# Loading v by heads over all 128 partitions, with key groups of eight units

## The chip, the cores and the metric

The kernel runs on one core of a Trainium2 chip. The metric is the device time of one execution in microseconds. Besides the times of plain executions there is one execution that the hardware profiler recorded; all views below come from it.

## The reference

Four batches, four heads, 1,088 positions, head size 32. Queries and keys go through a small feature map (two projections to 8 numbers and all 64 products of them), the attention is linear, and its result feeds one feed-forward layer with a swish whose slope `beta` is learned for each of 2,048 hidden units.

```python
def phi(x):                                   # 64 features of each position
    a = np.einsum('rd,bhsd->bhsr', S1, x)     # r = 8
    b = np.einsum('rd,bhsd->bhsr', S2, x)
    return np.einsum('bhsi,bhsj->bhsij', a, b).reshape(*x.shape[:-1], r * r)
q_p, k_p = phi(q), phi(k)
kv = np.einsum('bhsf,bhsd->bhfd', k_p, v)
z = np.sum(k_p, axis=2)
num = np.einsum('bhsf,bhfd->bhsd', q_p, kv)
den = np.einsum('bhsf,bhf->bhs', q_p, z)[..., None] + 1e-06
x = (num / den).transpose(0, 2, 1, 3).reshape(4 * 1088, 128)
h = x @ w_in                                  # 128 -> 2048
out = (h / (1 + np.exp(-beta * h))) @ w_out   # 2048 -> 128
```

## The kernel before

**Positions and units.** The 1,088 positions of a head are numbered as 32 rows (t) of 34 consecutive positions each; "unit" u of 0 to 33 is the u-th position of every row, so a unit is 32 positions of each head. q and k are loaded with heads and rows on the 128 partitions (L168 to L173), and VectorE (DVE) transposes them in blocks of 32 by 32 (L343, L348), after which unit u of all heads is a block of 32 columns in `kT` and `qT`. Column block 34 of `kT` is a pad of zeros.

**Key groups.** The sum over positions for kv wants positions on the partitions. The key projection (`k_project`, L353) therefore writes four groups of units to the four 32-partition quarters of a PSUM tile: `KU` gives the first unit of group j and `KN` how many it has (9, 9, 8, 8). It is one fp32 matmul per group and per half e of the heads, 8 in a batch, each of 9 x 32 = 288 columns; the ninth block of the two last groups is never used. `k_turn` (L365) transposes that into `tk`, the products of the two projections (`kp`, L370 to L383) are made on GpSimd (POOL) or DVE, and `kv_sum` (L515) adds v against them: for every column group c of 0 to 8 and every head h one fp32 matmul, over 128 partitions for c < 8 and over the first 64 for c = 8. v must lie as the key groups lie: partition 32 j + t, head h, column c holds row t of unit `KU[j] + c`. `load_v` (L175) does this with one load for each quarter j:

```python
KU = (0, 9, 18, 26)
KN = (9, 9, 8, 8)
```

Each is 32 partitions by 4 heads of one run of 1,152 or 1,024 bytes. Two buffers hold v: one for batch 0, one for batches 1 to 3.

**The rest of a batch.** `z_sum` (L385), the weights for the denominator (`w_project`, `w_mask`), the query projection, the denominator (`den_product` and what follows, L471 to L498), the query products (`qp`) and their turn (`qpt`), the kv tile turned to feed the numerator (`kvw`, `kvt`, `kvc` in batch 0; `kvo` and three small copies on SP's queue in the other batches), `num` (L560) and three copies into `xall` in fp16.

**The feed-forward stage** takes `xall` in chunks of up to 512 columns: steps `f<s>a/b` multiply by `winb` (w_in times beta, made on POOL by steps `wb0` to `wb3`, L310) into a PSUM wave, ScalarE (ACT) applies the swish, and steps `s<s>a/b` multiply by `woutp` (w_out over beta, steps `wo0` to `wo3`, L313). DVE transposes finished chunks and SP's queue stores them (`o0` to `o9`).

**Order.** Every step has a name, and one hand-written list, `ORDER`, sets in which order the steps are issued; each engine and each queue takes its own part of it in that order. `lv<b><j>` is the load of quarter j of v for batch b; `lk`, `lq`, `li`, `lo`, `lba` are the loads of k, q, w_in, w_out and the broadcast beta. All of these go out on SP's queue, S1, S2 and a small copy of beta on ACT's. Steps `i<n>` are n matmuls on zeros that keep TensorE (PE) running. For batch 0 the list has, on PE, `kpj0` (key projection), `zs0`, `qpjx0`, `cpjx0`, `kv00`, `i5`, `kv30 kv10 kv20`, `kvt0`, `i7`, `numx0`; on SP's queue `lk0a lk0b lq0a lv02 li0 lv00 lv01 lv03 lk11 lba1 li2 lk10 lba0 lo0 lq0b li1 lo1`.

Of the kernel before, what the change touches and what calls it, by code (L numbers as in the profile page):

```python
# [13 lines left out]
T = 32  # L14
# [3 lines left out]
def kernel(  # L18
# [12 lines left out]
    nc = tc.nc  # L31

    B, H, S, D = q.shape
# [5 lines left out]
    U = S // T  # L39
# [2 lines left out]


    NC = 9
    KU = (0, 9, 18, 26)
    KN = (9, 9, 8, 8)
    G = NC * H
    N = NC * T

# [1 line left out]

    ORDER = """
    lk0a ls2 lk0b lq0a ident pads warm i3 lv02 li0 lv00 ls1 lb i4 zms tbl lv01 sp kta0 masks ktb0 i2 sbd lv03
    qt0x0 kpj0 ktn0 sel kp10 sp2 kp30 bt i2 s2s lk11 lba1 li2 kp20 bc i3 kp00 zs0 lk10 zc0 qpjx0 wp0 wm0 i1 i2
    lba0 qtnx0 cpjx0 kv00 rb i5 ctnx0 kv30 kv10 kv20 kvw0 kvt0 dpx0 lo0 dsx0 drx0 anx0 qp00 lq0b li1 i7 kvc0 lo1
    qp10 qpt10 qpt00 lba3 lba2 ktb1 numx0 qt00 lq11 cpj0 lq10 xcx0 kta1 li3 qpj0 wb0 wo0 wb1 xax0 xbx0 wo1 i1
    f0a f0b ctn0 f1a qtn0 lo2 wb2 f1b lk21 dp0 lk20 ds0 kpj1 dr0 an0 f2a qp30 f2b s0a qp20 f3a f3b lv11 s0b s1a
    lo3 qt01 s1b s2a s2b lv13 qpt30 ktn1 qt11 wb3 f4a f4b f5a s3a qpt20 wo2 s3b f5b zs1 qpj1 qtn1 lv10 f6a zc1
    s4a wp1 wm1 f6b kp01 s4b wo3 num0 xb0 xc0 kta2 cpj1 xa0 lq20 f7a lq21 lv12 f7b kp21 s5a f8a kp31 s5b f8b
    ktb2 s6a ctn1 s6b s7a f9a kp11 f9b s7b lk30 f10a f10b kpj2 kv31 kv21 kv11 kv01 dp1 lk31 ds1 dr1 f11a f11b  # L60
    an1 qp21 o0 f12a s8a qt02 kvo1 f12b kr21 s8b kr31 ktn2 qp01 s9a s9b qpt21 qpt01 s10a f13a f13b s10b s11a
    qp11 qpt11 kr11 qt12 s11b f14a kp02 s12a f14b s12b f15a s13a lv23 s13b ktb3 f15b zs2 num1 zc2 lv21 s14a xc1
    s14b lq31 xa1 xb1 kp32 s15a lv20 lv22 s15b f16a f16b f17a kta3 wp2 f17b qpj2 wm2 cpj2 f18a f18b kp22 kp12
    qtn2 ctn2 f19a dp2 f19b lq30 kpj3 kv12 kv22 f20a o1 ds2 f20b dr2 s16a an2 f21a f21b kv02 qp02 kv32 f22a f22b
    s16b s17a f23a kvo2 f23b s17b s18a qpt02 s18b f24a f24b s19a kr22 s19b f25a qp12 f25b s20a s20b s21a lv30
    f26a f26b kr32 ktn3 qpt12 qp22 s21b s22a f27a f27b s22b s23a qpt22 s23b f28a f28b lv32 kr12 zs3 num2 zc3 xb2
    o2 wp3 xa2 f29a f29b xc2 lv31 s24a s24b kp33 f30a lv33 f30b s25a kp03 s25b qt13 s26a wm3 s26b f31a qt03 f31b
    s27a f32a f32b cpj3 qpj3 f33a f33b f34a s27b s28a f34b s28b s29a s29b f35a kp23 f35b s30a ctn3 s30b f36a
    qtn3 kp13 f36b dp3 ds3 s31a kv23 dr3 kv13 f37a f37b s31b o3 f38a an3 f38b kv03 qp13 kv33 f39a f39b kvo3 s32a
    s32b qp23 f40a kr23 f40b s33a s33b s34a f41a f41b kr13 qp03 s34b s35a f42a f42b s35b s36a s36b f43a kr33  # L70
    f43b s37a s37b qpt03 f44a f44b s38a qpt13 qpt23 s38b s39a f45a f45b s39b num3 xb3 o4 f46a f46b s40a xa3 xc3
    f47a f47b s40b s41a s41b f48a f48b s42a s42b f49a f49b s43a s43b f50a f50b s44a s44b s45a f51a f51b s45b
    s46a f52a f52b s46b s47a s47b f53a f53b f54a o5 xr f54b s48a s48b s49a f55a f55b s49b s50a f56a f56b s50b
    s51a f57a f57b s51b s52a s52b f58a f58b s53a s53b f59a f59b s54a s54b s55a s55b f60a f60b f61a o6 f61b s56a
    s56b s57a s57b f62a f62b s58a s58b f63a f63b s59a s59b o7 s60a f64a f64b s60b s61a f65a f65b s61b s62a s62b
    f66a f66b s63a s63b o8 f67a f67b s64a s64b s65a s65b s66a s66b s67a s67b o9
    """

    ENGINES = {
# [20 lines left out]
    def ct(shape, dtype, name):  # L100
        return const.tile(shape, dtype, tag=name, name=name)
# [6 lines left out]
    v_in = [v_two[0]] + [v_two[1]] * (B - 1)  # L108
# [17 lines left out]
    kT = ct([P, U + 1, T], F32, "kT")  # L126
    qT = ct([P, U + 2, T], F32, "qT")
    prods = [ct([P, G, R + 1], F32, f"prod{i}") for i in range(2)]
    sbd = ct([P, 2, 2 * R], F32, "sbd")
# [11 lines left out]
    st = [dict() for _ in range(B)]  # L141
# [3 lines left out]
    def step(name, f, *args):  # L145
        ops[name] = lambda: f(*args)
# [25 lines left out]

        nc.sync.dma_start(out=t[i:P:2, :], in_=rows[i:P:2, :])  # L173

    def load_v(b, j):  # L175
        nc.sync.dma_start(
            out=v_in[b][T * j : T * j + T, :, 0 : KN[j], :].rearrange("p h c d -> p h (c d)"),
            in_=bass.AP(
                tensor=v.tensor,
                offset=v.offset + b * H * S * D + KU[j] * D,  # L180
                ap=[[U * D, T], [S * D, H], [1, KN[j] * D]],
            ),
        )

    def load_w_in(i):
        nc.sync.dma_start(out=w_in_sb[:, i * 512 : i * 512 + 512], in_=moe_w_in[:, i * 512 : i * 512 + 512])
# [16 lines left out]
            step(f"lk{b}{i}", load_half, k_in[b], k_rows[b], i)  # L203
            step(f"lq{b}{i}", load_half, q_in[b], q_rows[b], i)
    for b in range(B):
        for j in range(4):
            step(f"lv{b}{j}", load_v, b, j)
    for i in range(4):
        step(f"li{i}", load_w_in, i)
        step(f"lo{i}", load_w_out, i)  # L210
# [142 lines left out]
    def k_project(b, js):  # L353
        st[b]["kpp"] = att2_t("kpp")
        for j in js:
            for e in range(2):
                nc.tensor.matmul(  # L357
                    out=st[b]["kpp"][T * j : T * j + T, e, 0:N],
                    lhsT=sbd[64 * e : 64 * e + 64, :, :].rearrange("p e r -> p (e r)"),
                    rhs=kT[64 * e : 64 * e + 64, KU[j] : KU[j] + NC, :].rearrange("p u t -> p (u t)"),  # L360
                    start=True,
                    stop=True,
                )

    def k_turn(b):  # L365
        tk = sb.tile([P, G, 2 * R], F32, tag="tk", name="tk")
# [229 lines left out]
    for b in range(B):  # L596
        step(f"kta{b}", k_transpose, b, 0, 18)
        step(f"ktb{b}", k_transpose, b, 18, U)
        step(f"kpj{b}", k_project, b, range(4))
        step(f"ktn{b}", k_turn, b)  # L600
        step(f"zs{b}", z_sum, b)
# [41 lines left out]
    u = 0  # L643
# [164 lines left out]
```

## Time and profile before

| | |
|---|---|
| median of 3 executions | 104.43 us (102.4 to 105.1) |
| the profiled execution | 103.5 us, span 101.8 us, granted TensorE clock 0.995 |
| PE busy | 95.1 us, 93% of the span |
| ACT, DVE, POOL busy | 72.3, 60.3, 40.6 us |
| DMA | 12.56 MB in 24,253 packets |
| v loads | 8 of 144 KB and 8 of 128 KB, 3.8 us from issue to landing at the median |
| first kv product | 10.44 us after the span's start |
| first feed-forward wave | 18.05 us |

The span is the part of the execution that the profile records; times in it count from its start. PE, ACT, DVE, POOL and SP are engines; "PEld" is the loading of weights into PE, beside its matmuls; an fp32 matmul shows as two records, one for each of two passes. The chain of waits follows the last work of the kernel back from step to step. A row of the stretches gives, after the two times, for PE, PEld, DVE, ACT and POOL the busy time and the number of instructions, then the granted clock, the busy share of the 16 DMA engines and GB/s.

### The profile page before, as it was taken

The numbers are of one execution on the slowest core, as the hardware profiler recorded it, in microseconds if no ns is written. First come the engines' busy times: TensorE is split into PE (matmuls) and PEld (weight loads), VectorE is DVE, ScalarE is ACT, GpSimd is POOL, SyncE is SP. The second block draws the span as 40 slices with busy tenths as digits, with TensorE's granted clock in tenths as the row PEclk, the third lists the DMA queues.
The fourth block names the chain that finished last, engine by engine and source line by source line (L and its number), as shares of the span: only waits on it lengthen the run. The fifth ranks groups of instructions, "written<-read, shape, count | busy, mean of one in ns | idle before, by whom it ended". The sixth has DMA issues, their size and how long they took to land.

```text
span 101.8 us, 3167 instructions
## 1 busy us (share of the span) xinstructions
PE 95.1 (93%) x1342; PEld 48.3 (47%) x1342; DVE 60.3 (59%) x110; ACT 72.3 (71%) x92; POOL 40.6 (40%) x49
## 2 busy tenths in 40 slices
PE   5999889999999999999999999999999999999940
PEld 1244454343545446345445534454444446689930
DVE  1574997999799894798983769189351040021110
ACT  1430022687587685788996788899969999989930
POOL 6419599769997996006272000068000000000000
PEclk9999999999999999999999999999999999999998
DMA  2999999981780627712440054034003205003421
GB/s 43 343 233 257 395 378 410 377 261 45 188 279 29 103 53 191 195 54 50 76 125 10 13 93 116 0 56 81 5 13 52 45 9 94 0 17 66 74 55 52
DMA packets 24253, 12.56 MB, mean 123 GB/s; under 512 B 17024, under 2 KB 21936, under 8 KB 24240
## 3 DMA queue, kind: packets, MB, share of 16 engines
q1 hardware_dynamic: 24032, 12.29, 44.7%
q8 instruction: 10, 0.16, 0.7%
q10 hardware_dynamic: 208, 0.08, 0.3%
q14 instruction: 3, 0.02, 0.1%
HBM read 9.84 MB, written 2.23 MB: 119 GB/s over the span
## 4 chain that ended last, share of the span: by engine, by line
PE 74%; DMA 8%; DVE 6%; ACT 5%; issue 1%; SPq 1%; ACTq 0%
PE wave L725 25%; PE acc L757 21%; PE at L520 6%; DMA v_in<-in_v_dram 6%; PE xp L571 5%; ACT gT L734 5%; PE fin L749 4%; DMA k_in<-in_k_dram 3%; PE idle L340 3%; PE qpp L430 3%; PE at L450 2%; PE at L393 2%; DVE prod L473 1%; PE kpp L357 1%; PE xw L571 1%
## 5 line engine op out<-in xcount | busy, mean ns | idle before, releaser
L734 ACT ACTIVATE gT<-wave 128x1024 f16<-128x1024 f32 (+1 forms) x69 | 65.8, 1011 | 8.5 <-PE wave L725 7.9
L725 PE MATMUL wave<-xall,winb 128*128 128x512 f16 (+1 forms) x128 | 36.1, 366 | 0.4 <-DVE xall L588 0.2
L757 PE MATMUL acc<-gT,woutp 128*128 128x512 f16 (+1 forms) x128 | 34.7, 366 | 0.0
L372 POOL TENSOR_TENSOR qp<-an,tq 128x768 f32<-128x768 f32 (+1 forms) x8 | 14.0, 1760 | 23.1 <-DVE an L496 23.1
L725 PEld LDWEIGHTS <-winb 128*128 128x128 f16 x160 | 14.8, 99 | 16.1 <-issue 4.3
L757 PEld LDWEIGHTS <-woutp 128*128 128x128 f16 x128 | 12.4, 97 | 12.9 <-issue 0.4
L372 POOL TENSOR_TENSOR kp<-tk 128x512 f32<-128x512 f32 (+1 forms) x12 | 15.0, 1273 | 6.0 <-DVE tk L368 6.0
L684 DVE STREAM_TRANSPOSE osb<-acc 128x512 f32<-128x512 f32 (+1 forms) x8 | 5.4, 680 | 17.7 <-PE acc L757 14.8
L508 DVE STREAM_TRANSPOSE qpt<-qp 128x768 f32<-128x768 f32 (+1 forms) x13 | 11.1, 883 | 0.3 <-POOL qp L372 0.2
L340 PE MATMUL idle<-warm 128*128 128x512 f16 x30 | 9.4, 450 | 1.3 <-DVE tiny L231 1.3
L344 DVE STREAM_TRANSPOSE kT<-k_in 128x576 f32<-128x576 f32 (+1 forms) x8 | 5.6, 722 | 2.4 <-DMA k_in<-in_k_dram 2.4
L571 PE MATMUL xp<-qpt,kvr 32*32 32x288 f32 (+2 forms) x160 | 6.9, 364 | 0.0
L571 PE MATMUL xw<-qpt,kvr 32*32 32x256 f32 (+1 forms) x160 | 6.8, 343 | 0.0
L520 PE MATMUL at<-kp,v_in 128*32 128x64 f32 (+1 forms) x288 | 6.3, 223 | 0.3 <-DMA v_in<-in_v_dram 0.3
L520 PEld LDWEIGHTS at<-kp,v_in 128*32 128x32 f32 (+1 forms) x288 | 4.6, 109 | 3.8 <-issue 2.7
L349 DVE STREAM_TRANSPOSE qT<-q_in 128x512 f32<-128x512 f32 (+1 forms) x8 | 5.8, 725 | 0.8 <-DMA q_in<-in_q_dram 0.7
L310 POOL TENSOR_TENSOR winb<-w_in_sb,beta_all 128x512 f16<-128x512 f32 x4 | 5.1, 1276 | 0.0
L340 PEld LDWEIGHTS <-warm 128*128 128x128 f16 x30 | 2.9, 111 | 4.5 <-issue 1.6
L473 DVE TENSOR_TENSOR prod<-tq,tcc 128x288 f32<-128x288 f32 (+2 forms) x5 | 4.9, 985 | 0.1
L571 PEld LDWEIGHTS xp<-qpt,kvr 32*32 32x32 f32 x160 | 3.7, 103 | 2.3 <-issue 0.8
L725 PE MATMUL wave<-xlast,winb 128*128 128x256 f16 x32 | 4.7, 272 | 0.0
L372 DVE TENSOR_TENSOR qp<-an,tq 128x768 f32<-128x768 f32 (+1 forms) x5 | 4.5, 906 | 0.1
(76 smaller groups left out, 73.4 us busy)
## 6 DMA issues: line engine op xcount, KB each, us to landing
k_in<-in_k_dram SPq DMA_DIRECT2D x6, 272.0 KB, 4.9
q_in<-in_q_dram SPq DMA_DIRECT2D x6, 272.0 KB, 4.6
v_in<-in_v_dram SPq DMA_DIRECT2D x8, 144.0 KB, 3.8
v_in<-in_v_dram SPq DMA_DIRECT2D x8, 128.0 KB, 3.8
w_in_sb<-in_moe_w_in_dram SPq DMA_DIRECT2D x4, 256.0 KB, 5.4
beta_all<-in_moe_beta_dram SPq DMA_DIRECT2D x4, 256.0 KB, 6.0
w_out_sb<-in_moe_w_out_dram SPq DMA_DIRECT2D x4, 256.0 KB, 5.5
out_dram<-osb SPq DMA_DIRECT2D x16, 64.0 KB, 1.9
```

Of the source, the lines that this page charges most:

```text
L340: nc.tensor.matmul(out=t[:, 0, :], lhsT=warm[:, 0:P], rhs=warm, start=True, stop=True)
L344: nc.vector.transpose(out=kT[:, u0:u1, :].rearrange("p u t -> p (u t)"), in_=k_in[b][:, u0 * D : u1 * D])
L349: nc.vector.transpose(out=qT[:, u0:u1, :].rearrange("p u t -> p (u t)"), in_=q_in[b][:, u0 * D : u1 * D])
L372: eng.tensor_tensor(out=ap(o, g0 * F, [[F, n], [R, R], [1, R]]), in0=ap(a, g0 * a_step + a_off, [[a_step, n], [1, R], [0, R]]), in1=ap(bsr ...
L473: nc.vector.tensor_tensor(out=prods[b % 2][:, g0 : g0 + n, 0:R], in0=ap(st[b]["tq"], g0 * 2 * R, [[2 * R, n], [1, R]]), in1=st[b]["tcc"][: ...
L508: nc.vector.transpose(out=ap(st[b]["qpt"], c0 * H * F, [[1, (c1 - c0) * H * F]]), in_=ap(st[b]["qp"], c0 * H * F, [[1, (c1 - c0) * H * F]]),)
L520: nc.tensor.matmul(out=t[T * h : T * h + T, :], lhsT=v_in[b][:n, h, c, :], rhs=kp[:n, 4 * c + h, :], start=(done == 0), stop=(done == NC - 1),
L571: nc.tensor.matmul(out=ts[j][T * h : T * h + T, 0 : n * T], lhsT=st[b]["kvr"][p : p + T, f, h, :], rhs=ap(st[b]["qpt"], (4 * c0 + h) * F + ...
L684: nc.vector.transpose(out=osb[:, :un, :].rearrange("p u m -> p (u m)"), in_=accs[ci][:, : un * T])
L725: nc.tensor.matmul(out=wvs[s][:, w, i * n : i * n + n], lhsT=winb[:, j * P : j * P + P], rhs=xlast[:, u0 * T - LAST0 :][:, :n] if ci in tu ...
L734: nc.scalar.activation(out=g[:, o + i * 512 : o + i * 512 + 1024 // m], in_=wvs[s].rearrange("p a n -> p (a n)")[:, i * 512 : i * 512 + 10 ...
L757: nc.tensor.matmul(out=accs[ci][:, :n], lhsT=woutp[:, j, :], rhs=gts[s // GP][:, o : o + n], start=(j == 0), stop=(j == NJ - 1),)
```

## The change

The key groups become 8 consecutive units each, 8 j to 8 j + 7, for column groups 0 to 7; the two units that are left, 32 and 33, form column group 8 of quarters 0 and 1. v follows: a load per head fills all 128 partitions with runs of 1,024 bytes, and two small loads put units 32 and 33 into column group 8, 32 partitions by 4 heads of 128 bytes each. A batch has six v loads instead of four. `lv<b>0` to `lv<b>3` now name heads and keep their places in the order; `lv<b>4` and `lv<b>5` follow the fourth of them (`lv14 lv15` behind `lv12`, `lv24 lv25` behind `lv22`, `lv34 lv35` behind `lv33`); nothing else in the order differs. The key projection makes two matmuls for each group and half: 256 columns, and 32 columns for column group 8 (from the zero pad for quarters 2 and 3).

```diff
-    KU = (0, 9, 18, 26)
-    KN = (9, 9, 8, 8)
+    KG = 8
...
-    lk0a ls2 lk0b lq0a ident pads warm i3 lv02 li0 lv00 ls1 lb i4 zms tbl lv01 sp kta0 masks ktb0 i2 sbd lv03
-    qt0x0 kpj0 ktn0 sel kp10 sp2 kp30 bt i2 s2s lk11 lba1 li2 kp20 bc i3 kp00 zs0 lk10 zc0 qpjx0 wp0 wm0 i1 i2
+    lk0a ls2 lk0b lq0a ident pads warm i3 lv02 li0 lv00 ls1 lb i4 zms tbl lv01 sp kta0 masks ktb0 i2 sbd lv03
+    lv04 lv05 qt0x0 kpj0 ktn0 sel kp10 sp2 kp30 bt i2 s2s lk11 lba1 li2 kp20 bc i3 kp00 zs0 lk10 zc0 qpjx0 wp0
...
-    def load_v(b, j):
-        nc.sync.dma_start(
-            out=v_in[b][T * j : T * j + T, :, 0 : KN[j], :].rearrange("p h c d -> p h (c d)"),
-            in_=bass.AP(
-                tensor=v.tensor,
-                offset=v.offset + b * H * S * D + KU[j] * D,
-                ap=[[U * D, T], [S * D, H], [1, KN[j] * D]],
-            ),
-        )
+    def load_v(b, h):
+
+        if h < H:
+            nc.sync.dma_start(
+                out=v_in[b][:, h, 0:KG, :].rearrange("p c d -> p (c d)"),
+                in_=bass.AP(
+                    tensor=v.tensor,
+                    offset=v.offset + (b * H + h) * S * D,
+                    ap=[[KG * D, 4], [U * D, T], [1, KG * D]],
+                ),
+            )
+        else:
+            j = h - H
+            nc.sync.dma_start(
+                out=v_in[b][T * j : T * j + T, :, KG, :],
+                in_=bass.AP(
+                    tensor=v.tensor,
+                    offset=v.offset + b * H * S * D + (4 * KG + j) * D,
+                    ap=[[U * D, T], [S * D, H], [1, D]],
+                ),
+            )
...
     for b in range(B):
-        for j in range(4):
-            step(f"lv{b}{j}", load_v, b, j)
+        for h in range(H + 2):
+            step(f"lv{b}{h}", load_v, b, h)
...
         for j in js:
             for e in range(2):
-                nc.tensor.matmul(
-                    out=st[b]["kpp"][T * j : T * j + T, e, 0:N],
-                    lhsT=sbd[64 * e : 64 * e + 64, :, :].rearrange("p e r -> p (e r)"),
-                    rhs=kT[64 * e : 64 * e + 64, KU[j] : KU[j] + NC, :].rearrange("p u t -> p (u t)"),
-                    start=True,
-                    stop=True,
-                )
+                for u0, c0, n in ((KG * j, 0, KG), (4 * KG + min(j, 2), KG, 1)):
+                    nc.tensor.matmul(
+                        out=st[b]["kpp"][T * j : T * j + T, e, c0 * T : (c0 + n) * T],
+                        lhsT=sbd[64 * e : 64 * e + 64, :, :].rearrange("p e r -> p (e r)"),
+                        rhs=kT[64 * e : 64 * e + 64, u0 : u0 + n, :].rearrange("p u t -> p (u t)"),
+                        start=True,
+                        stop=True,
+                    )
```

More of the change, by code (lines that the diff above doesn't have):

```diff
@@ L53 @@
     lk0a ls2 lk0b lq0a ident pads warm i3 lv02 li0 lv00 ls1 lb i4 zms tbl lv01 sp kta0 masks ktb0 i2 sbd lv03
-    qt0x0 kpj0 ktn0 sel kp10 sp2 kp30 bt i2 s2s lk11 lba1 li2 kp20 bc i3 kp00 zs0 lk10 zc0 qpjx0 wp0 wm0 i1 i2
-    lba0 qtnx0 cpjx0 kv00 rb i5 ctnx0 kv30 kv10 kv20 kvw0 kvt0 dpx0 lo0 dsx0 drx0 anx0 qp00 lq0b li1 i7 kvc0 lo1
-    qp10 qpt10 qpt00 lba3 lba2 ktb1 numx0 qt00 lq11 cpj0 lq10 xcx0 kta1 li3 qpj0 wb0 wo0 wb1 xax0 xbx0 wo1 i1
-    f0a f0b ctn0 f1a qtn0 lo2 wb2 f1b lk21 dp0 lk20 ds0 kpj1 dr0 an0 f2a qp30 f2b s0a qp20 f3a f3b lv11 s0b s1a
@@ L58 @@
[L58 to L76, printed above, removed]
+    lv04 lv05 qt0x0 kpj0 ktn0 sel kp10 sp2 kp30 bt i2 s2s lk11 lba1 li2 kp20 bc i3 kp00 zs0 lk10 zc0 qpjx0 wp0
@@ new lines @@
+    wm0 i1 i2 lba0 qtnx0 cpjx0 kv00 rb i5 ctnx0 kv30 kv10 kv20 kvw0 kvt0 dpx0 lo0 dsx0 drx0 anx0 qp00 lq0b li1
+    i7 kvc0 lo1 qp10 qpt10 qpt00 lba3 lba2 ktb1 numx0 qt00 lq11 cpj0 lq10 xcx0 kta1 li3 qpj0 wb0 wo0 wb1 xax0
+    xbx0 wo1 i1 f0a f0b ctn0 f1a qtn0 lo2 wb2 f1b lk21 dp0 lk20 ds0 kpj1 dr0 an0 f2a qp30 f2b s0a qp20 f3a f3b
+    lv11 s0b s1a lo3 qt01 s1b s2a s2b lv13 qpt30 ktn1 qt11 wb3 f4a f4b f5a s3a qpt20 wo2 s3b f5b zs1 qpj1 qtn1
+    lv10 f6a zc1 s4a wp1 wm1 f6b kp01 s4b wo3 num0 xb0 xc0 kta2 cpj1 xa0 lq20 f7a lq21 lv12 lv14 lv15 f7b kp21
@@ new lines @@
+    s5a f8a kp31 s5b f8b ktb2 s6a ctn1 s6b s7a f9a kp11 f9b s7b lk30 f10a f10b kpj2 kv31 kv21 kv11 kv01 dp1 lk31
+    ds1 dr1 f11a f11b an1 qp21 o0 f12a s8a qt02 kvo1 f12b kr21 s8b kr31 ktn2 qp01 s9a s9b qpt21 qpt01 s10a f13a
+    f13b s10b s11a qp11 qpt11 kr11 qt12 s11b f14a kp02 s12a f14b s12b f15a s13a lv23 s13b ktb3 f15b zs2 num1 zc2
+    lv21 s14a xc1 s14b lq31 xa1 xb1 kp32 s15a lv20 lv22 lv24 lv25 s15b f16a f16b f17a kta3 wp2 f17b qpj2 wm2
+    cpj2 f18a f18b kp22 kp12 qtn2 ctn2 f19a dp2 f19b lq30 kpj3 kv12 kv22 f20a o1 ds2 f20b dr2 s16a an2 f21a f21b
@@ new lines @@
+    kv02 qp02 kv32 f22a f22b s16b s17a f23a kvo2 f23b s17b s18a qpt02 s18b f24a f24b s19a kr22 s19b f25a qp12
+    f25b s20a s20b s21a lv30 f26a f26b kr32 ktn3 qpt12 qp22 s21b s22a f27a f27b s22b s23a qpt22 s23b f28a f28b
+    lv32 kr12 zs3 num2 zc3 xb2 o2 wp3 xa2 f29a f29b xc2 lv31 s24a s24b kp33 f30a lv33 lv34 lv35 f30b s25a kp03
+    s25b qt13 s26a wm3 s26b f31a qt03 f31b s27a f32a f32b cpj3 qpj3 f33a f33b f34a s27b s28a f34b s28b s29a s29b
+    f35a kp23 f35b s30a ctn3 s30b f36a qtn3 kp13 f36b dp3 ds3 s31a kv23 dr3 kv13 f37a f37b s31b o3 f38a an3 f38b
@@ new lines @@
+    kv03 qp13 kv33 f39a f39b kvo3 s32a s32b qp23 f40a kr23 f40b s33a s33b s34a f41a f41b kr13 qp03 s34b s35a
+    f42a f42b s35b s36a s36b f43a kr33 f43b s37a s37b qpt03 f44a f44b s38a qpt13 qpt23 s38b s39a f45a f45b s39b
+    num3 xb3 o4 f46a f46b s40a xa3 xc3 f47a f47b s40b s41a s41b f48a f48b s42a s42b f49a f49b s43a s43b f50a
+    f50b s44a s44b s45a f51a f51b s45b s46a f52a f52b s46b s47a s47b f53a f53b f54a o5 xr f54b s48a s48b s49a
+    f55a f55b s49b s50a f56a f56b s50b s51a f57a f57b s51b s52a s52b f58a f58b s53a s53b f59a f59b s54a s54b
@@ L77 @@
+    s55a s55b f60a f60b f61a o6 f61b s56a s56b s57a s57b f62a f62b s58a s58b f63a f63b s59a s59b o7 s60a f64a
+    f64b s60b s61a f65a f65b s61b s62a s62b f66a f66b s63a s63b o8 f67a f67b s64a s64b s65a s65b s66a s66b s67a
+    s67b o9
     """
```

## The prediction

> **What bounds the kernel now.** I read the page first, then the chain of waits in its opening part, then the instructions in order of time on SP's queue and on TensorE (PE) up to 19 us, then the busy time by stretches.
>
> ```profile
> span 101.8 us, 3167 instructions
> PE 95.1 (93%) x1342; PEld 48.3 (47%) x1342; DVE 60.3 (59%) x110; ACT 72.3 (71%) x92; POOL 40.6 (40%) x49
> PE 74%; DMA 8%; DVE 6%; ACT 5%; issue 1%; SPq 1%; ACTq 0%
> ```
>
> PE is busy 93% of the span and holds 74% of the chain that ended last; the 8% of DMA in that chain lie at the start. From 18 us on PE has almost no gap, so a delay of the start is not made up later: what is late at 18 us ends late.
>
> ```profile
> 3.63 0.72 SPq L176
> 4.40 5.79 DMA v_in<-in_v_dram
> 10.44 0.43 PE at L520 x16
> 10.87 1.19 PE idle L340 x5
> 12.06 1.24 PE at L520 x56
> ```
>
> The chain runs over the last v load of batch 0 (lv03): issued at 4.40, landed at 4.40 + 5.79 = 10.19 us. The first kv products (L520) start right behind it; on their own row PE had waited 0.35 us. The copies, kv turn, numerator and first wave (18.05 us) follow.
>
> ```profile
> 0.00:2.50 2.50, 1.24 (x3) 0.43 (x4) 0.28 (x2) 0.37 (x1) 1.62 (x15) 1.00 0.24 41
> 2.50:5.00 2.50, 2.50 (x15) 0.78 (x13) 1.36 (x3) 1.12 (x2) 1.16 (x7) 1.00 1.01 344
> 5.00:7.50 2.50, 2.50 (x27) 1.10 (x25) 1.75 (x5) 0.78 (x5) 0.19 (x1) 1.00 1.03 230
> 7.50:10.00 2.50, 2.46 (x67) 1.15 (x65) 1.14 (x4) 0.28 (x3) 2.50 (x2) 1.00 1.05 245
> 10.00:12.50 2.50, 2.15 (x49) 1.13 (x45) 2.18 (x5) 0.00 (x0) 1.37 (x2) 1.00 1.07 399
> ```
>
> The last two columns are the busy share of the 16 DMA engines and GB/s. From 2.5 us they are full; while the v loads go through (5 to 10 us) they move 230 to 245 GB/s, against 344 before and 399 behind. So v into 32 partitions at a time runs slowly, and that is the room for a gain.
>
> ```profile
> SPq L169 <- DMA v_in<-in_v_dram: 0.6, 1, 0.6
> SPq L189 <- DMA v_in<-in_v_dram: 0.5, 1, 0.5
> 7.89 0.33 SPq L214 DMA_DIRECT2D beta_all<-in_moe_beta_dram  x1
> 8.76 0.39 SPq L189 DMA_DIRECT2D w_out_sb<-in_moe_w_out_dram  x1
> 9.72 0.34 SPq L169 DMA_DIRECT2D q_in<-in_q_dram  x1
> ```
>
> SP, too, waits for v: lo0 goes out at 8.76 when lv00 has landed, lq0b at 9.72 when lv01 has. Counted along the queue, a load waits for the one eight places earlier; eight are outstanding at most.
>
> ```profile
> q1 hardware_dynamic: 24032, 12.29, 44.7%
> q10 hardware_dynamic: 208, 0.08, 0.3%
> ```
>
> q10 (ACT's queue) is worth counting out. It carries S1 and S2 (8 rows each), beta (16 rows) and one final store (128 rows): 160 data packets. The other 48 are 4-byte completion writes: 16 for beta, 16 for the store, 8 each for the S loads. A transfer whose outermost count is 8 thus runs on 8 DMA engines, not 16.
>
> **The change part by part.** *The four head loads.* Bytes stay the same. Before, both sides of a v load walk 32 outermost rows. After, SBUF walks 128 partitions, but the DRAM side is [4, 32, 256 elements] with 4 outermost; the strides (1,024 bytes against 4,352) don't merge. No transfer of before has two different counts, so the trace leaves two answers: 16 engines as now, or 4. By the S loads the count of engines follows the outermost count, and a cut by the DRAM side's outer loop gives 4; I take 4. The Trainium skill, "DMA: Bandwidth & Descriptors", section "Why a DMA increments its semaphore by 16 and not by 1", says it outright: the largest number up to 16 that divides the outermost counts of both sides, and on SP's queue the lowest-numbered engines. The S loads agree with it; its answer for 4 against 128 no run here shows yet.
>
> On 4 engines each takes 32 packets of 1,024 bytes per load. In the packet records such a packet took 46 ns at the median where traffic was light and 65 ns at the median (82 at the upper quartile) in batch 0's v loads. Only 4 engines are crowded now, so I take 55 ns: 32 x 0.055 = 1.76 us a load, 7.04 for four. Landing events put lq0a, ahead of v, at 5.01 us (median engine); li0 stands between the v loads at 0.64; the two small loads add 2 x 8 x 13 ns = 0.21 (128-byte packets, median 11 to 13 ns). So v is there at 5.01 + 7.04 + 0.64 + 0.21 = 12.9 us against 10.19: **+2.7 us**. Bounds: at 46 ns 11.75 (+1.6), at 82 ns 16.4 (+6.2); on 16 engines at 344 to 399 GB/s a gain, worked out below.
>
> What is late next: lv00 to lv03 are all needed by kv00 (one head each), then five idle matmuls, kv30, kv10, kv20, kvw, kvt, kvc, num, the x copies and the first wave stand behind it in PE's and ACT's order. The k products (POOL, done at 11.37) stop being a cover. Everything behind v on the same four engines is late by the same amount: lk11, lba1, li2, lk10 and lba0 add 0.97 + 0.61 + 0.64 + 0.67 + 0.62 (landing steps), so lba0 lands near 16.4 instead of 13.04, and wb0 on POOL (14.09) moves by 2.3; lq0b lands near 17.9 instead of 15.54, and qt00 on DVE by 2.4. All three arms that meet before the first wave move by about as much; I add none to another.
>
> *Later batches.* v of batch 3 (lv31, lv33) is issued at 59.78 and 60.26 behind eight stores, first packets at 60.9, landed at 64.08; kv23 uses it at 64.46. Two loads of 1.76 us plus 0.2 and a landing of 0.25 end at 64.9: 0.4 us of waiting. Batch 2 lands at 42.95 and is used at 45.05; two loads that take 1.4 us more each would miss that by up to 0.7, batch 1 has about 2 us. PE runs in order, but waves ahead of the kv sums can cover some: I take **+0.5 us** for all three (0 to 3).
>
> *The two small loads* add two issues a batch, 0.47 us apart, ahead of lk11, lba1, li2, lk10, lba0, lo0, lq0b and so on, and use two of the eight places. SP is ahead of full engines, so this costs 0 here; with the cover gone, 0.95. In batches 1 to 3 they stand before f7b, s15b and f30b, ahead of lk30, lq30 and the stores; SP's next waits there are for DVE's osb, so 0. kv30 and the last sum of each batch newly wait for them, behind the head loads.
>
> *The key projection* (L357). 8 fp32 products of 288 columns become 8 of 256 and 8 of 32, so 16 more PE records and weight loads a batch. Today 16 records take 0.71 us: the first passes of eight products start 7 ns apart (5.420 to 5.467), their second passes 267 ns later; eight array tiles work side by side. Streaming per tile stays 288 columns; kv records of 64 columns follow each other on a tile at 56 ns, so 2 x 32 columns cost 0 to 0.1 us: **+0.1 us** for four batches (0 to 0.4). Products j = 0 and 1 newly need units 32 and 33, the second transpose half; in batch 0 that ends at 5.06 while L357 waits for sbd until 5.13, so 0.
>
> **Sum**: 2.7 + 0.5 + 0.1 = +3.3 us. The profiled execution took 103.5 (span 101.8, 1.7 around it), so 106.8 there; it lies 0.9 below the shown median of 104.43 (runs 102.4 to 105.1), against which I forecast: 104.4 + 3.3 = **107.7 us**.
>
> **Rivals.**
> - *Sixteen engines.* Four loads of 128 KB at the step of a full-rate 256 KB load (0.64) take 4 x 0.32 + 0.2 = 1.5 us of queue instead of 2.8. For it: both sides have 128 rows in all, and today's v loads are visibly slow. But PE waits only 0.35 us for v, and wb0 waits for POOL until 14.09 anyway. Gain 0.3 to 1.3, about 0.6: 103.8 us. It decides from the point at which v lands before 10.1 us. Chance 0.16.
> - *Four engines, at the light-traffic pace.* 46 ns and covered later batches: +1.6, less what slack there is, 105.7. For it: packets of 46 ns in batches 1 to 3. Chance 0.15.
> - *Four engines, each step stalls.* At 82 ns v lands at 16.4 (+6.2 at most), and batches 2 and 3 wait too: +6, 110.4. Against it: 12 engines stand aside. Chance 0.10.
> - *The small products block the projection.* If each waits for the 256-column product on its tile and holds the next tile's back, the side-by-side is lost: 8 products x 2 passes x 0.267 = 4.3 us instead of 0.7, 3.6 a batch. Batch 0 hides it behind the late v; the other three make 10.8: 104.4 + 3.3 + 10.8 = 118.5. Against it: second-pass weights load from 5.447, before the last first passes have started at 5.467, so one tile's second pass holds nothing back. "TensorE: Matmul & The Clock Gate", Part 3, in the Trainium skill has matmuls start and end strictly in program order; that would be this case, and the records speak against it. Chance 0.03.
>
> **How the numbers follow.** The forecast has 0.56, with a range of its own of 106.0 to 109.8. The whole range, 103.7 to 110.6, takes in most of the first two rivals and of the third. A measurement of this kernel tells about 2% (2.1 us) from no change: slower from 106.5 on. Slower: 0.52 of the forecast, 0.10 and 0.03 of the two slow rivals, 0.05 of the light pace, 0.70. Faster needs 102.3, more than the 16-engine case gives at its middle: 0.07 of its 0.16. Within 2%: 0.04 + 0.10 + 0.09 = 0.23.
>
> **What would show it.** Right: completion writes of 4 instead of 16 on the head loads, so 24,992 packets on q1: today's 24,032 hold 1,600 completions (100 transfers of 16) and 22,432 data packets; the change adds 1,024 data packets (8 small loads of 128), and 92 transfers complete with 16, 16 with 4. With 16 engines it would be 25,184. The first L520 near 13, wb0 near 16.4, the first wave near 20.7, GB/s between 5 and 12 us well below 230, DMA share far under 1. L357 still near 0.7 us for 32 records. Wrong: L520 before 10.4 with 300 GB/s or more (16 engines), or L357 at 2 us and more.

## The result, and the profile after

The changed kernel takes 110.08 us at the median (four runs, 109.33 to 111.88), the kernel before beside it on the same chip 103.76 (102.4 to 105.1). The ratio is 1.064, with a 95% interval of 1.057 to 1.071: slower, by 6.3 us where 3.3 were forecast. The profiled execution of the changed kernel ran at a lower granted clock (0.953 on average) than its other three (0.984 to 1.0) and is the longest of them, so what it shows of the clock is told apart below; ratios leave out executions more than 1.5% above the fastest of their kernel, medians do not.

The opening part of its page:

```profile
span 110.1 us, 3305 instructions
PE 100.5 (91%) x1406; PEld 52.4 (48%) x1406; DVE 58.4 (53%) x110; ACT 72.3 (66%) x92; POOL 40.7 (37%) x49
PEclk9999555599999999999999999999999999999999
q1 hardware_dynamic: 24992, 12.29, 40.5%
PE 57%; DMA 21%; ACT 7%; DVE 5%; SPq 5%; issue 1%; ACTq 0%
```

Read the last line against that of before: DMA's share of the chain that ended last rises from 8% to 21%, PE's falls from 74% to 57%. The queue line holds exactly the 24,992 packets worked out for completion writes of 4. The clock line is in no step of the prediction: half speed in four of the forty slices, from 11 to 22 us.

The chain of waits names the places (start, length, what):

```profile
4.72 8.14 DMA v_in<-in_v_dram
12.90 0.63 PE at L533 x10
13.53 2.25 PE idle L352 x5
15.78 2.01 PE at L533 x56
18.23 1.22 PE at L561 x4
19.45 2.72 PE idle L352 x7
...
45.23 6.31 DMA v_in<-in_v_dram
...
57.98 4.27 DMA kvr<-kvr
...
67.94 4.64 DMA v_in<-in_v_dram
```

Before, the chain held one v load, 5.79 us in batch 0, and no copy. Now it has four such pieces: v of batch 0 (landed at 12.86 instead of 10.19), v of batch 2, a copy of the turned kv (`kvr`), and v of batch 3. The second group of lines is the clock: the same five idle matmuls took 1.19 us before and take 2.25, the 56 kv products 1.24 and now 2.01.

The busy time by stretches (PE, PEld, DVE, ACT, POOL, then granted clock, DMA share, GB/s):

```profile
2.50:5.00 2.50, 2.50 (x15) 0.78 (x13) 1.28 (x2) 1.12 (x2) 1.16 (x7) 1.00 0.97 338
5.00:7.50 2.50, 2.50 (x43) 1.59 (x41) 2.03 (x5) 0.89 (x5) 0.44 (x1) 1.00 0.30 96
7.50:10.00 2.50, 2.46 (x68) 1.19 (x67) 0.88 (x4) 0.17 (x1) 2.50 (x2) 1.00 0.61 172
10.00:12.50 2.50, 0.69 (x6) 0.28 (x6) 2.31 (x6) 0.00 (x0) 1.32 (x3) 0.81 0.94 296
12.50:15.00 2.50, 2.10 (x14) 0.97 (x15) 1.86 (x3) 0.00 (x0) 1.37 (x1) 0.50 0.85 285
```

From 5 to 7.5 us only 30% of the 16 engines are busy and 96 GB/s move, where the share was 1.03 and 230 GB/s moved. Twelve of the engines have nothing of v. The landing events of the trace, one for each engine that has finished its share of a transfer, show it: four report each head load. The small load issued right behind v (lv04) was finished by twelve engines at 8.27, by the other four between 12.34 and 13.03, behind v. The twelve go on with later loads, which is why the share climbs again before v has landed.

From 10 to 12.5 us PE is busy 0.69 of 2.5 us: it waits for v.

```profile
11.54 0.43 PE L533 MATMUL at<-kp,v_in 128*32 128x64 f32 x4 [1.29 <-DMA v_in<-in_v_dram]
12.90 0.63 PE L533 MATMUL at<-kp,v_in 128*32 128x64 f32 x10 [0.92 <-DMA v_in<-in_v_dram]
```

The first kv products start at 9.96 already, not near 13 as was named, since each load now brings one head and the products of the first head need only that one; PE then waits 1.29 us for the second and 0.92 for the last. The clock stands at 0.50 from 12.5 us on.

SP's queue while batch 2 hands over to batch 3 (start, length, DMA issue), and the third copy before:

```profile
55.39 0.59 SPq L551 DMA_DIRECT2D kvr<-kvr  x1
56.08 0.56 SPq L178 DMA_DIRECT2D v_in<-in_v_dram  x1
56.70 0.57 SPq L551 DMA_DIRECT2D kvr<-kvr  x1
57.36 0.56 SPq L178 DMA_DIRECT2D v_in<-in_v_dram  x1
57.98 0.56 SPq L551 DMA_DIRECT2D kvr<-kvr  x1
```

```profile
51.34 0.51 SPq L538 DMA_DIRECT2D kvr<-kvr  x1
```

Two v loads (lv30, lv32) lie between three small copies. Before, the third copy was issued at 51.34 and the last engine had finished it at 53.43, in 2.1 us; now it takes 4.27, and the numerator of batch 2 (L584) waits for it. Again twelve engines are done early, by 60.06; the other four end between 61.76 and 62.25, right behind lv32, whose four events stand at 61.58 to 62.07. This wait is in no step of the prediction.

### The profile page after: what moved, and what is told of

It is laid out like the page before. It is cut to its first block, busy times and chain, and to the rows that moved or that the text cites. A ratio compares the mean times of both kernels' runs of the same rounds, so it can differ in the third digit from the quotient of the medians.

```text
span 110.1 us, 3305 instructions
## 1 busy us (share of the span) xinstructions
PE 100.5 (91%) x1406; PEld 52.4 (48%) x1406; DVE 58.4 (53%) x110; ACT 72.3 (66%) x92; POOL 40.7 (37%) x49
## 3 DMA queue, kind: packets, MB, share of 16 engines
q1 hardware_dynamic: 24992, 12.29, 40.5%
## 4 chain that ended last, share of the span: by engine, by line
PE 57%; DMA 21%; ACT 7%; DVE 5%; SPq 5%; issue 1%; ACTq 0%
PE wave L738 18%; DMA v_in<-in_v_dram 17%; PE acc L770 15%; PE at L533 6%; ACT gT L747 6%; PE idle L352 5%; DMA kvr<-kvr 4%; PE xp L584 4%; PE fin L762 3%; SPq L178 3%; DVE qpt L521 2%; PE at L463 1%; PE xw L584 1%; SPq L169 1%; PE at L561 1%
## 5 line engine op out<-in xcount | busy, mean ns | idle before, releaser
L352 PE MATMUL idle<-warm 128*128 128x512 f16 x30 | 11.5, 530 | 1.3 <-DVE tiny L243 1.3
L533 PE MATMUL at<-kp,v_in 128*32 128x64 f32 (+1 forms) x288 | 8.6, 245 | 2.8 <-DMA v_in<-in_v_dram 2.7
L533 PEld LDWEIGHTS at<-kp,v_in 128*32 128x32 f32 (+1 forms) x288 | 5.9, 121 | 6.7 <-DMA v_in<-in_v_dram 3.8
L584 PE MATMUL xp<-qpt,kvr 32*32 32x288 f32 (+2 forms) x160 | 7.6, 364 | 0.5 <-DMA kvr<-kvr 0.5
L584 PE MATMUL xw<-qpt,kvr 32*32 32x256 f32 (+1 forms) x160 | 6.7, 343 | 0.0
L352 PEld LDWEIGHTS <-warm 128*128 128x128 f16 x30 | 3.5, 129 | 5.9 <-issue 4.0
L584 PEld LDWEIGHTS xp<-qpt,kvr 32*32 32x32 f32 x160 | 3.8, 103 | 3.4 <-DMA kvr<-kvr 1.1
L601 ACT CAST xall<-xw 128x128 f16<-128x128 f32 (+1 forms) x8 | 2.4, 325 | 4.3 <-PE xw L584 3.3
L474 DVE STREAM_TRANSPOSE tcc<-at 128x288 f32<-128x288 f32 (+1 forms) x4 | 1.8, 439 | 6.0 <-PE at L463 6.0
```

The costliest lines, as they stand in the source:

```text
L352: nc.tensor.matmul(out=t[:, 0, :], lhsT=warm[:, 0:P], rhs=warm, start=True, stop=True)
L533: nc.tensor.matmul(out=t[T * h : T * h + T, :], lhsT=v_in[b][:n, h, c, :], rhs=kp[:n, 4 * c + h, :], start=(done == 0), stop=(done == NC - 1),
L584: nc.tensor.matmul(out=ts[j][T * h : T * h + T, 0 : n * T], lhsT=st[b]["kvr"][p : p + T, f, h, :], rhs=ap(st[b]["qpt"], (4 * c0 + h) * F + ...
```

## The experiments

All are edits of the changed kernel, except three that start from the kernel before, which say so. Ratios are to the kernel before on the same chip.

**The same kernel once more**, to see whether the profile repeats.

> The changed kernel once more, for a profile in which TensorE keeps its clock. Theory A (the head loads run on 4 DMA engines): 24,992 packets on q1 again, first L533 within 0.5 us of 12.9, the first wave between 20.5 and 22, span 107 to 108.7. Theory C (the loss is mostly the halved clock behind the wait): with the granted clock at 0.98 or more over the span, the first wave comes before 20 and the span is under 106.

Measured: 110.72 us, span 108.9 (just above the range), again 24,992 packets, v landed at 13.51, the first wave at 23.2 (later than named), again a clock of 0.5 to 0.6 between 11 and 19 us, 0.962 over the span. What follows: the packet count and the late v are the kernel's, not one execution's. The fall of the clock came again, but whether it comes and how long it lasts differ: over the four executions above the clock was 0.953, 0.984, 0.984 and 1.0.

**The same four loads with the rows outermost.** Same bytes and run lengths, all 128 partitions; only which DRAM dimension is walked first differs. v then lies on other partitions than the keys it belongs to, so kv is another sum.

```
-  ap=[[KG * D, 4], [U * D, T], [1, KG * D]],
+  ap=[[U * D, T], [KG * D, 4], [1, KG * D]],
```

> The changed kernel with one difference: the DRAM side of a head load walks the 32 rows outermost and the 4 groups inside. Bytes, runs of 1,024 bytes, number of loads and their places stay; v comes to lie on other partitions, so the output is not the reference's. Theory A (the outermost count of 4 sets the number of DMA engines): q1 has 25,184 packets, v of batch 0 lands before 10.2 us, and the time is that of the kernel before or up to 1 us less, 102.8 to 104.2. Theory B (six loads a batch, the small packets, the places in the queue and the split projection cost the time): it stays 2 to 6 us above the kernel before.

Measured: 104.42 us, ratio 1.0115 [1.0089, 1.0142], 25,184 packets on q1 (16 engines). Its queue line, stretches, chain and a wait:

```profile
q1 hardware_dynamic: 25184, 12.29, 43.7%
...
5.00:7.50 2.50, 2.50 (x42) 1.49 (x41) 1.78 (x5) 0.59 (x4) 0.12 (x1) 1.00 0.79 252
7.50:10.00 2.50, 2.46 (x66) 1.20 (x68) 1.20 (x4) 0.47 (x4) 2.50 (x2) 1.00 0.90 219
10.00:12.50 2.50, 2.50 (x73) 1.45 (x71) 2.01 (x5) 0.00 (x0) 1.44 (x2) 1.00 0.94 289
...
9.86 6.51 DMA q_in<-in_q_dram
...
PE at L463 <- DVE qT L361: 0.6, 1, 0.6
```

v has landed at 8.29 and the first kv product starts at 10.10; PE doesn't wait for v, and the clock stays at 1.00. What follows: one line of the access pattern is worth 5.2% of the time (1.064 against 1.012). But the 1.2% that is left, a little more than was expected, shows that 16 engines would not have made the change a gain either. A part of it is seen here: with v early, q comes late. Its second half lands at 16.37 (15.54 before), PE waits 0.6 us for its transpose (`qT`), and the first wave is 0.2 us later than before.

**Eight outermost.** The source is cut so that 8 chunks are walked outermost; other elements of v are read, of the same number and run length.

```
-  ap=[[KG * D, 4], [U * D, T], [1, KG * D]],
+  ap=[[4 * U * D, 8], [KG * D, 16], [1, KG * D]],
```

> The changed kernel with the DRAM side of a head load walked as 8 outermost steps of 16 runs of 1,024 bytes; number, size and places of the loads stay, other elements of v are read, so the output is not the reference's. If the outermost count sets the number of DMA engines: 8 completion writes a load, 25,056 packets on q1 (24,992 at 4 engines, 25,184 at 16); 16 packets of 55 ns an engine, 0.88 us a load, so v of batch 0 lands by 5.0 + 0.64 + 3.5 + 0.2 = 9.4 us, before PE asks for it, and 103.8 to 105.2 us. If something else in the shape of the load is slow: 106 or more.

Measured: 104.45 us, ratio 1.012 [1.0079, 1.0162].

```profile
q1 hardware_dynamic: 25056, 12.29, 43.6%
```

These 25,056 packets are 92 x 16 + 16 x 8 completions and 23,456 data packets. v has landed at 9.73 and the first kv product starts at 9.76. What follows: with 4, 8 and 32 outermost against 128 partitions, 4, 8 and 16 engines carry the load. And the time is not proportional to their number: from 4 to 8 engines 5.2% are won, from 8 to 16 nothing, because with 8 v lands just when PE is ready for it. Here, too, q is late (16.86): PE waits 1.4 us for its transpose, and the first wave is 0.7 us later than before.

**Four loads by quarters**, as before, with the two small loads and the new key groups kept.

```
-  out=v_in[b][:, h, 0:KG, :].rearrange("p c d -> p (c d)"),
+  out=v_in[b][T * h : T * h + T, :, 0:KG, :].rearrange("p h c d -> p h (c d)"),
...
-  offset=v.offset + (b * H + h) * S * D,
-  ap=[[KG * D, 4], [U * D, T], [1, KG * D]],
+  offset=v.offset + b * H * S * D + h * KG * D,
+  ap=[[U * D, T], [S * D, H], [1, KG * D]],
```

> The changed kernel with its key groups of 8, its two small loads and its split projection, but the four large loads by quarters as before: 32 partitions by 4 heads of 1,024 bytes. Theory A: 25,184 packets on q1 and 103.5 to 104.8 us, that is 0 to 1 above the kernel before for the two small loads and the split. Theory B: 2 to 6 us above it.

Measured: 103.97 us, ratio 1.0081 [1.0048, 1.0113]. What follows: everything in the change but the head loads costs 0.8%; the head loads cost the rest.

**The split projection alone**, in the kernel before: each fp32 product of 288 columns becomes one of 256 and one of 32.

```
+  for u0, c0, n in ((KU[j], 0, NC - 1), (KU[j] + NC - 1, NC - 1, 1)):
...
-      rhs=kT[64 * e : 64 * e + 64, KU[j] : KU[j] + NC, :].rearrange("p u t -> p (u t)"),
+      rhs=kT[64 * e : 64 * e + 64, u0 : u0 + n, :].rearrange("p u t -> p (u t)"),
```

> The kernel before with one difference: each key projection product of 288 columns is made as one of 256 and one of 32. Prediction's step: 32 records of the projection in about 0.7 us, total 0 to 0.4 us more. Rival (each small product waits for the large one on its array tile and holds the next back): the projection takes 4.3 us and the kernel is some 11 us slower.

Measured: 103.56 us, ratio 0.9986 [0.9943, 1.003]. The group of the projection (count, busy us, mean ns), before and here:

```profile
L357 PE MATMUL kpp<-kT,sbd 64*32 64x288 f32 x64 | 2.9, 415 | 0.0
L358 PE MATMUL kpp<-kT,sbd 64*32 64x256 f32 (+1 forms) x128 | 3.1, 289 | 0.0
```

Twice as many records add 0.2 us of busy time, and nothing measurable to the end. The products on different array tiles still run side by side: in batch 0 the first passes of the eight large products start between 5.25 and 5.35 us, the small ones that stand between them in the program only from 5.71 on. What follows: the rival of blocked products is dead. Its sum of 118.5 had rested on a strict order of matmuls; the rule of the Trainium skill for that ("TensorE: Matmul & The Clock Gate", Part 3) does not hold here across array tiles, by these starts and by 3.1 us against the 17.2 (4 x 4.3) that the rival gives a strict order.

**By heads in batch 0 alone**, by quarters in the other three:

```
+  if b == 0:
       # the load by heads
+  else:
+      # the load by quarters, as above
```

> The changed kernel, but only batch 0 loads v by heads (4 engines); batches 1 to 3 load the same groups by quarters as in the quarters experiment (103.97 us). Theory D (the loss has parts: v of batch 0 lands 2.7 us late, TensorE's clock falls to half behind the wait, and later batches lose some 2 us): 107.3 to 109.0 us, first L533 pass ending near 13.5 us and a granted clock below 1 between 10 and 22 us. Theory E (the later batches carry most of the loss): 104.5 to 106.

Measured: 107.61 us, ratio 1.0447 [1.0408, 1.0486]. Its chain:

```profile
4.72 8.63 DMA v_in<-in_v_dram
...
14.03 2.25 PE idle L362 x5
```

**By heads in batches 1 to 3 alone** (the test is `b > 0`):

> The opposite: batch 0 by quarters, batches 1 to 3 by heads. Theory D: 105.4 to 107.0 us, with the granted clock at 1.00 in the first 22 us and num of batch 2 waiting for the last of the small kvr copies. Theory E: 107.5 to 109. Should batches 1 to 3 hide their loads, as the prediction's 0.5 us had it: 104.0 to 104.8.

Measured: 106.4 us, ratio 1.0307 [1.026, 1.0354]. Its chain (of an execution of 108.93 us) has no load of batch 0, and these two DMA pieces in the middle:

```profile
42.04 6.90 DMA v_in<-in_v_dram
55.38 4.40 DMA kvr<-kvr
```

What follows from the two: above the 0.8% of the quarters, batch 0 costs 3.7% and the other three together 2.3%. With the 0.8% that makes 6.7%, against 6.4% measured for all: the parts nearly add. The later batches, forecast at 0.5 us, cost 2.3% of 103, about 2.3 us.

**Keeping PE busy while it waits**: eleven idle matmuls ahead of the first kv products, so that the clock stays up. If the fall of the clock were a large part of the loss, this should win it back.

```
-  ... lba0 qtnx0 cpjx0 kv00 rb i5 ...
+  ... lba0 qtnx0 cpjx0 i11 kv00 rb i5 ...
```

> The changed kernel with 11 more idle matmuls ahead of kv00, so that TensorE works instead of waiting for v. If the halved clock is a part of the loss: clock 1.00 in the stretches from 10 to 22 us, i5, the kv sums and i7 back at 1.2, 1.3 and 1.7 us, the first wave between 20.5 and 21.5, and 106 to 108.5 us. If it is not (the loads alone set the first wave): 109.5 to 110.5 as before.

Measured: 109.73 us (109.18 to 110.49), ratio 1.0651 [1.0591, 1.0711]. The clock line of its page, and its chain:

```profile
PEclk9999999999999999999999999999999999999999
```

```profile
4.69 8.81 DMA v_in<-in_v_dram
13.54 0.41 PE at L533 x10
13.95 1.19 PE idle L352 x5
15.13 1.24 PE at L533 x56
...
16.82 0.71 PE at L561 x4
```

The mechanism is real: the idle matmuls are back at 1.19 us and the kv products at 1.24. But it is no large part of the loss: the ratio is that of the changed kernel, and the time is that of the second case named. What follows: the slowed clock made one profiled execution longer (first wave at 24.27, here at 21.13), but it isn't what made the median slower. This kernel is the undisturbed view of the change. Against before its waves start 3.1 us late, 3.3 before the kv sums of batch 2, 4.2 behind them, 5.15 behind the numerator of batch 2, 5.7 behind the kv sums of batch 3, and the span is 5.7 longer (107.5 us).

**The three copies ahead of v of batch 3** (lv30 and lv32 moved behind the last copy):

```
-  ... s21a lv30 f26a f26b kr32 ... f28b lv32 kr12 zs3 num2 ...
+  ... s21a f26a f26b kr32 ... f28b kr12 lv30 lv32 zs3 num2 ...
```

> The changed kernel with lv30 and lv32 moved in the order to behind the last of batch 2's three kvr copies. If those copies queue behind the head loads on the same DMA engines: the third copy lands 1.8 to 2.2 us after its issue instead of 4.3, num of batch 2 no longer waits for it, and the kernel is 1 to 2 us faster than the changed one, 108.0 to 109.3. If the copies are not on the path: 109.5 to 110.5.

Measured: 110.9 us (109.45 and 109.78; 112.02 and 112.12 at a granted clock of 0.954), ratio 1.0635 [1.0582, 1.0688]: no gain. In its profile the third copy takes 1.84 us, as expected, and the wait for the copies is gone (the numerator starts at 58.68 without one). The waits of this kernel, its chain, and a line of the chain of the kernel with the idle matmuls:

```profile
PEld at L533 <- DMA v_in<-in_v_dram: 5.2, 6, 1.3
PE at L533 <- DMA v_in<-in_v_dram: 4.0, 5, 1.1
```

```profile
42.53 6.61 DMA v_in<-in_v_dram
65.51 4.75 DMA v_in<-in_v_dram
```

```profile
65.49 4.67 DMA v_in<-in_v_dram
```

PE waits 4.0 us for v in all, against 2.7 in the changed kernel: its waves fall back 1.7 us at the kv sums of batch 3, where the kernel with the idle matmuls loses 0.9 at the copies and 0.6 at v. What follows: the wait for the copies only hid a part of the next wait. The last head load of batch 3 (lv33) stands in SP's queue behind eight stores. It was issued at 65.51 and landed at 70.25, in the kernel with the idle matmuls at 65.49 and 70.16, although PE was 1.0 us further on here. PE needs that landing in either kernel, whether it has waited for the copies or not.

**The same move in the kernel before**, as its control:

> The kernel before with lv30 and lv32 moved behind the last of batch 2's kvr copies. With 16-engine loads the copies are held up little (1.9 us from issue to landing already): within 0.5% either way, -0.5 to +0.5 us. A gain of over 0.5% would make this the fastest version.

Measured: 103.46 us, ratio 1.003 [0.9996, 1.0064]. What follows: with 16 engines the order of these loads and copies changes nothing that these runs can tell.

**The two small loads alone**, in the kernel before: two loads of 16 KB a batch, in runs of 128 bytes, at the places of lv04 and lv05, into a tile that nobody reads.

```
+  for b in range(B):
+      for j in range(2):
+          step(f"lv{b}{4 + j}", load_small, b, j)
```

> The kernel before with two more loads of 16 KB a batch, at the places of the changed kernel's small ones, into a tile that nothing reads. The 16-engine variants stood 0.8 and 1.2% above the kernel before. If the small loads make that: 0.5 to 1.3% slower here. If they cost nothing, as the prediction's sum had it: within 0.3%, and the rest is due to waiting on them or to the head loads' own shape.

Measured: 104.87 us, ratio 1.013 [1.006, 1.02]. What follows: they aren't free (here they read 1% more bytes, in the changed kernel they don't). With the 1.0081 of the quarters and the 1.0115 and 1.012 of the two kernels on more engines, they could account for what is left when the 4-engine walk is taken out. Where they cost it stays open: the profiled execution, 103.83 us, shows 0.3 us in the span, and q isn't late in it (its transpose starts at 15.59, 15.56 before).

**The change on 16 engines, with the keys in v's order**: rows outermost as above, and the projection reading its key columns in the order that v then has.

```
-  for u0, c0, n in ((KG * j, 0, KG), (4 * KG + min(j, 2), KG, 1)):
+  for c0, n, cols in (
+      (0, KG, ap(kT, 8 * j, [[T, KG], [1, 8], [KG * T, 4]], 64 * e, 64)),
+      (KG, 1, kT[64 * e : 64 * e + 64, 4 * KG + min(j, 2), :]),
+  ):
...
-  rhs=kT[64 * e : 64 * e + 64, u0 : u0 + n, :].rearrange("p u t -> p (u t)"),
+  rhs=cols,
```

> Head loads over 128 partitions done on 16 engines with the right output: the DRAM side walks rows outermost as in the rows-first experiment (104.42 us), and the key projection reads kT in the same order (column b of group j is row 8j + b // 4 of unit 8 (b % 4) + c), so the products match v again. If PE reads the strided columns at full speed: 103.9 to 105.0 us, as the rows-first experiment. If the strided reads slow the projection (L370 well over 0.7 us a batch): 105 to 108.

Measured: 104.61 us, ratio 1.016 [1.0116, 1.0203]. Its projection:

```profile
L373 PE MATMUL kpp<-kT,sbd 64*32 64x256 f32 (+1 forms) x128 | 4.8, 401 | 0.0
```

What follows: it mends most of the loss and is better than the changed kernel, but not than the one before. The columns read in strides make the projection 4.8 us busy in place of 3.1 (the time stays in the range named for full speed all the same). Here, too, q lands late (16.87), and the first wave is 0.75 us later than before. No version tried is measurably faster than the kernel before.

## Why the prediction was right, and where its terms were off

*The direction and the mechanism were right.* 24,992 packets, 30% of the DMA engines, and a v that landed at 12.86 (worked out: 12.9, with the small loads, which landed at 13.22). In five executions with this load of batch 0 it landed between 12.86 and 13.51. From lq0a (4.86 at the median engine) to lv03 a load takes (12.86 - 4.86 - 0.64) / 4 = 1.84 us; 1.76 was taken. A single packet took 46 ns at the median and 49 to 55 on average in these executions, at most the 55 that were estimated. A part of the time thus lies between the packets, for which the step had no term: that the total came out so close is in part luck. The Trainium skill ("DMA: Bandwidth & Descriptors", "Why a DMA increments its semaphore by 16 and not by 1") gives 4 engines for counts of 128 and 4, and the three kernels with 4, 8 and 16 agree with it.

*What follows v at the start was right.* wb0 came at 16.19 (16.4), qt00 at 17.62 (17.9). The first wave starts at 20.70 in the kernel with the copies first, whose clock was 0.994, and at 21.13 with the idle matmuls; 20.7 had been named. In these two v landed at 12.88 and 13.50. So the term of +2.7 us measured 2.65 to 3.1.

*"Later batches: +0.5 us" is the term that failed.* By the undisturbed waves it is 5.7 - 3.1 = 2.6 us: 1.0 for v of batch 2, 0.9 for the copies of batch 2, 0.6 for v of batch 3, and 0.2 ahead of these. Three things were wrong in that step. It read the landing of v of batch 2 as 42.95; the last landing event stands at 43.29, and with it the step's own working (2.8 us more, against 45.05 - 43.29) gives the 1.0 that was measured. It had named up to 0.7 and 0.4 for the two v waits and then cut them, since waves ahead of the sums might cover some; they covered nothing, as PE takes the steps of the list in order and before had no gap over 0.03 us from 24 to 76 us. And it looked at v alone: the copies follow lv30 and lv32 in SP's queue, and on the four engines of v they ended right behind these loads, 2 us after the other twelve had finished them. The bound of 0 to 3 held it.

*"The small loads cost 0 here"* was too low: alone they cost 1.3% [0.6, 2.0], together with the new key groups 0.8% [0.5, 1.1], about 1 us. The step had 0.95 for the case that SP's lead is gone. That in the three kernels with an early v it is q, behind the small loads, that lands 0.8 to 1.3 us late fits this case; whether the small loads make it late was not tested, and in the kernel before, where q isn't late, the reason is open.

*"The projection: +0.1"* was right: 0.2 us of busy time and a ratio of 0.9986.

*The median.* 110.08 lies inside the whole range of 103.7 to 110.6 but above the forecast's own, 106.0 to 109.8. It equals, to 0.3 us, the rival in which each step stalls, but not by that rival's mechanism: v did not land at 16.4. Only its other half, the waits of batches 2 and 3, took place. The slowed clock was in no rival; with it held up, the loss is still 6.5% [5.9, 7.1]. That is 6.7 us at the median, where the profiled executions differ by 5.7; where the last 1.0 us lies no profile shows.

*The supposed gain* was bounded well by "PE waits only 0.35 us for v". The slow 230 GB/s of the loads into 32 partitions was no lever: with 16 engines over 128 partitions the first kv product starts at 10.10 instead of 10.44, and the kernel is still 1% slower.

## What to carry to other kernels

Look at the outermost count on both sides of a DMA before its partitions, its bytes or its run length: 4 chunks outermost against 128 partitions left 4 of 16 engines to carry it, and the order of two dimensions in one line was worth 5% of the kernel. When a load gets slower, price each transfer behind it on the same engines, not only those who read it: the copies behind v of batch 3 cost PE 0.9 us, v of batch 2 itself 1.0. And before a wait is taken out, look at what the next one waits for: here it was a load that landed at the same time in both orders, so the time was only moved.

## What the hardware showed that was not expected

- **The clock behind a wait.** PE had 0.69 us of work in the 2.5 us up to 12.5, and the granted clock fell to 0.50 for 10.24 us. In the same kernel once more it fell for 6.83 us, and for 3.41 with heads in batch 0 alone; these are 3, 2 and 1 times 3.41. With eleven idle matmuls in the gap it stayed at 1.00. It also stayed there in the profile of the kernel with the copies first, where PE had 0.60 us of work in the same 2.5 us, so the wait alone doesn't decide it. While the clock is down the five idle matmuls take 2.25 instead of 1.19 us.
- **A small copy behind a narrow load.** The third `kvr` copy went from 2.1 to 4.27 us (3.94 and 4.40 in two other kernels); twelve engines had finished it in 2.1 us, the four of the load ahead of it ended last.
- **Small loads count.** Eight loads of 16 KB, 1% of the bytes, cost 1.3% [0.6, 2.0] by the median, though the profiled execution shows only 0.3 us.
- **Columns in strides.** The same 128 fp32 records of the projection took 401 ns on average with columns read in strides, against 289.
